# Transposing normalized activations by DMA in place of TensorE in a fused local-attention and gated-MLP kernel

## The chip, the core and the metric

The kernel runs on one core of a Trainium2 chip. A core has a matrix engine (TensorE, PE in the profile, with its weight loads as PEld), a vector engine (VectorE, DVE), an activation engine (ScalarE, ACT), GpSimd (POOL) and SyncE (SP), which here only issues DMAs. Each engine takes its own instructions strictly in order; semaphores order the engines against one another. The metric is the time of one execution on the device in microseconds, the median of several runs.

## What is computed

Input x has 2048 rows of 1024 values (bf16). Each row is normalized (xn), and xn goes through two branches: an attention with 32 heads of 32 values, in which each position looks at 8 earlier positions at distances 0, 2, ..., 14, and a gated MLP of width 3584. The result is x + s * silu(MLP).

```python
def reference(A_x, A_wqkv, A_wo, B_x, B_w1, B_w3, B_w2):
    ...
        qkv = (lambda x, *d: x.transpose(*d))((x @ wqkv).reshape(B, S, 3, H, Dh), 2, 0, 3, 1, 4)
    ...
        logits = jnp.einsum("bhsd,bhswd->bhsw", q, kg) * scale
        logits = jnp.where(mask[None, None, :, :], logits, -1e9)
        attn = _softmax(logits, axis=-1)
        o = jnp.einsum("bhsw,bhswd->bhsd", attn, vg)
    ...
        h = _silu(gate) * up
        out = jnp.einsum("bsf,fd->bsd", h, w2)
    ...
    x = A_x
    xn = _layernorm(x, axis=-1)
    s = _A_ref(xn, A_wqkv, A_wo)
    g = _silu(_B_ref(xn, B_w1, B_w3, B_w2))
    return x + s * g
```

## The kernel before

The 2048 rows are worked on in four chunks of 512 rows (c = 0 to 3), each of four tiles of 128 rows. TensorE contracts over the partition axis, so xn is needed transposed: the tile xnT holds, for each of the 8 blocks of 128 model columns, 128 partitions (columns) by 512 rows. There are two xnT buffers.

For each chunk the program text has these steps, in this order:

- `qkv` (line 143): 24 blocks of queries, keys and values, 8 matmuls each (line 159), with weights wt streamed from a permuted copy wperm in device memory; in chunk 0 they come from tiles pm that were permuted on the chip. ScalarE copies the results to qT, kT and vT (line 170).
- `attention` (line 172): VectorE multiplies qT with shifted kT, once per distance, and adds up (lines 177 to 180); GpSimd's DMAs regroup the sums (line 184); a softmax follows (lines 188 to 201); its result goes back by DMA (line 204); VectorE multiplies it with shifted vT and adds up to oT (lines 211 to 226).
- `wo_proj` (line 229): 64 matmuls of oT with the output weights wa and wb (line 241), copied to s_sb by ScalarE.
- `mlp_up` (line 250): 14 blocks fb of 256 columns. Each loads w1t and w3t (lines 255 and 257) and makes four PSUM tiles of 8 matmuls each (line 264, named gu_fb_k); ScalarE applies Silu to the gate (sg, line 271) and VectorE multiplies it with the other half (ht, line 273). That product frees the PSUM tiles; the pool psum_mm has six.
- `ln_transpose` (line 112) for the next chunk, c + 1: SyncE loads four tiles x_t (line 122, four buffers), VectorE makes the statistics (lines 125 and 126), ScalarE a square root (line 129), VectorE the reciprocal (line 130) and then xn, tile by tile (line 133, two buffers). TensorE transposes each xn tile in eight blocks of 128 columns into a PSUM tile tp (line 139; tp shares a pool of two buffers with wo_proj), and ScalarE copies tp to xnT (line 140).
- `mlp_down_epilogue` (line 294): for each half of the output columns, 112 matmuls into four accumulators (line 324), with w2t streamed through three buffers (line 320), and then the final Silu, product and sum (lines 289 to 292). The last half of chunk 3 has its own order (line 311).

Chunk 0 differs in that its `ln_transpose` runs first of all, tile by tile, and that its first four MLP blocks are made before the loop (lines 332 to 338).

The program text does not fix the order on the engines. A scheduler places each engine's instructions at build time: of those that it takes to be ready, it picks the one that stands earliest in the text (or is marked high priority), and it lets later work move far ahead when its inputs and a buffer are there. That order is then fixed, and an instruction whose input is late on the chip holds all that stand behind it on its engine. All weight and x_t loads are issued by SyncE, in one queue; GpSimd issues the attention's DMAs, x_e and the output.

Of the kernel before, what the change touches and what calls it, by code (L numbers as in the profile page):

```python
# [15 lines left out]
def kernel(  # L16
# [11 lines left out]
    nc = tc.nc  # L28
    P = 128
# [40 lines left out]
    for _ in range(NWARM):  # L70
# [4 lines left out]
        out=ident[:], in_=ident[:], compare_op=ALU.not_equal, fill=1.0,  # L75
# [5 lines left out]
        out=maskb[0:32], in_=maskb[0:32], compare_op=ALU.is_ge, fill=-1.0e9,  # L81
# [30 lines left out]
    def ln_transpose(c, group=NST):  # L112
        xnT = xnT_pool.tile([P, KT, CH], BF16, tag="xnT")
        mv = small.tile([P, NST, nc.vector.BN_AGGR_DIM], FP32, tag="mv")
        rstd = small.tile([P, NST], FP32, tag="rstd")
        for st0 in range(0, NST, group):
            sts = range(st0, st0 + group)
            x_ts = {}
            for st in sts:
                g = c * NST + st  # L120
                x_t = ln.tile([P, D], BF16, tag="x_t", bufs=NST)
                nc.sync.dma_start(out=x_t[:], in_=x_flat[g * P:(g + 1) * P, :])
                stats = small.tile([P, 2, nc.vector.BN_STATS_DIM], FP32, tag="stats")
                for i in range(2):
                    nc.vector.bn_stats(out=stats[:, i, :], in_=x_t[:, i * 512:(i + 1) * 512])  # L125
                nc.vector.bn_aggr(out=mv[:, st, :], in_=stats[:])
                x_ts[st] = x_t
            sl = slice(st0, st0 + group)
            nc.scalar.activation(out=rstd[:, sl], in_=mv[:, sl, 1], func=ACTF.Sqrt, bias=eps_t[:], scale=1.0)
            nc.vector.reciprocal(out=rstd[:, sl], in_=rstd[:, sl])  # L130
            for st in sts:
                xn = ln.tile([P, D], BF16, tag="xn")
                nc.vector.tensor_scalar(
                    out=xn[:], in0=x_ts[st][:], scalar1=mv[:, st, 0:1], scalar2=rstd[:, st:st + 1],
                    op0=ALU.subtract, op1=ALU.mult,
                )
                tp = psum_aux.tile([P, KT, P], BF16, tag="aux")
                for kt in range(KT):
                    nc.tensor.transpose(tp[:, kt, :], xn[:, kt * P:(kt + 1) * P], ident[:])  # L139
                nc.scalar.copy(out=xnT[:, :, st * P:(st + 1) * P], in_=tp[:])  # L140
        return xnT
# [188 lines left out]

    pools = {}
    xnT_cur = ln_transpose(0, group=1)
    hts0 = []
    with tc.tile_pool(name="stage", bufs=1) as stage:
# [4 lines left out]
        for t in range(3):  # L339
            nc.sync.dma_start(  # L340
                out=wperm[:, :, t * NJ:(t + 1) * NJ, :].rearrange("kt kp j p -> kp kt (j p)"),
                in_=pms[t][:].rearrange("kp kt j p -> kp kt (j p)"),
# [9 lines left out]
    for c in range(NCH):  # L352
        if c > 0:
            qkv(c, xnT_cur)
        oT = attention(c)
        s_sb = wo_proj(c, oT)
        if c == 0:
            hts = hts0 + mlp_up(c, xnT_cur, M1B, FT // 2)
        else:
            hts = mlp_up(c, xnT_cur, 0, FT // 2)  # L360
        xnT_next = ln_transpose(c + 1) if c + 1 < NCH else None
        mlp_down_epilogue(c, hts, s_sb)
        xnT_cur = xnT_next
# [30 lines left out]
```

## Time and profile before

| | us |
|---|---|
| median of 3 runs | 841.57 |
| lowest and highest run | 841.38 and 841.77 |
| span of the profiled execution | 841.2 |
| chunk 0 up to the end of its qkv | 0 to 62.6 |
| rest of chunk 0, up to the first line 159 of chunk 1 | 62.6 to 223.7 (161.1) |
| chunk 1 | 223.7 to 427.0 (203.3) |
| chunk 2 | 427.0 to 630.2 (203.2) |
| chunk 3 | 630.2 to 841.2 (211.0) |

The parts overlap on the other engines; they are cut where TensorE begins the projections of the next chunk. The profile is of one execution. In lines of the timeline the columns are start and duration in microseconds, engine, line of the kernel, operation, output<-input, tile shapes and a count; in brackets is the time that the engine stood idle before, and what ended it. "SPq" and "POOLq" are the queues in which these engines issue DMAs; a duration there is the time that the issue holds the queue, and the transfer goes on behind it ("landing" counts from the issue to the last byte).

### The profile page before, as it was taken

How to read it: one execution, taken by the hardware profiler on the slowest of the kernel's cores; microseconds unless marked ns; L12 is line 12 of the kernel's file. 1: busy time of each engine (PE TensorE's matmuls, PEld its weight loads, DVE VectorE, ACT ScalarE, POOL GpSimd, SP SyncE). 2: the span in 40 equal slices, each digit the busy share in tenths (PEclk: the TensorE clock that was granted, in tenths of full speed). 3: DMA queues.
4: the chain of work that ended last, by engine and by line, in shares of the span. 5: the costliest groups of instructions: out<-in, count | busy, mean ns of one | idle time of the engine just before them, and what ended most of it. 6: DMA issues, size and time to landing. Idle time of an engine off the chain costs nothing.

```text
span 841.2 us, 9707 instructions
## 1 busy us (share of the span) xinstructions
PE 819.3 (97%) x3884; PEld 377.0 (45%) x3884; DVE 477.1 (57%) x488; ACT 213.9 (25%) x325; POOL 123.7 (15%) x210
## 2 busy tenths in 40 slices
PE   7999889999999999999999999999999999999995
PEld 5444334444444444444444444444444444444442
DVE  7429946595239835494143955379302693629811
ACT  6742113103343113102233212210403311310120
POOL 1002133003100224002120040401102004120011
PEclk8999999999999999999999999999999999999998
DMA  9999397746595596754675577855476559593320
GB/s 302 314 358 230 102 226 173 190 150 176 130 289 149 153 201 183 177 164 119 193 239 150 148 170 185 202 154 167 114 213 200 151 150 200 159 205 112 109 81 25
DMA packets 208525, 149.54 MB, mean 178 GB/s; under 512 B 7776, under 2 KB 196192, under 8 KB 208480
## 3 DMA queue, kind: packets, MB, share of 16 engines
q1 hardware_dynamic: 201296, 132.14, 57.2%
q0 software_dynamic: 7184, 16.79, 8.0%
q8 instruction: 30, 0.49, 0.3%
q14 instruction: 15, 0.12, 0.1%
HBM read 130.02 MB, written 10.49 MB: 167 GB/s over the span
## 4 chain that ended last, share of the span: by engine, by line
PE 80%; DVE 15%; issue 3%; DMA 1%; ACT 0%; POOL 0%; POOLq 0%; DVEq 0%
PE ps L159 20%; PE ps L241 7%; DVE oT L226 2%; DVE B L225 2%; DVE C L211 2%; DVE B L211 2%; DVE ht L273 1%; DVE prod L177 1%; DMA x_t<-in_A_x_dram 1%; PE tp L139 1%; DVE oT L219 1%; PE acc_1_3_1668 L324 1%; PE acc_1_2_6323 L311 1%; PE acc_1_0_4763 L324 1%; PE acc_0_2_1505 L324 1%
## 5 line engine op out<-in xcount | busy, mean ns | idle before, releaser
L264 PEld LDWEIGHTS <-w3t 128*128 128x128 bf16 x912 | 89.8, 98 | 111.4 <-issue 7.8
L264 PEld LDWEIGHTS <-w1t 128*128 128x128 bf16 x912 | 89.6, 98 | 104.6 <-issue 0.2
L159 PE MATMUL ps<-xnT,wt 128*128 128x512 bf16 x576 | 124.8, 379 | 0.0
L324 PEld LDWEIGHTS <-ht 128*128 128x128 bf16 x784 | 76.4, 98 | 90.0 <-issue 0.2
L177 DVE TENSOR_TENSOR prod<-qT,kT 128x4096 bf16<-128x4096 bf16 x32 | 72.6, 2286 | 41.8 <-ACT kT L170 40.9
L159 PEld LDWEIGHTS <-wt 128*128 128x128 bf16 x576 | 56.3, 98 | 68.0
L290 DVE TENSOR_TENSOR gt<-gt,s_sb 128x512 f32<-128x512 f32 (+1 forms) x33 | 21.6, 673 | 77.0 <-ACT gt L289 64.3
L125 DVE BATCH_NORM_STATS2 stats<-x_t 128x6 f32<-128x512 bf16 x32 | 20.5, 671 | 58.4 <-DMA x_t<-in_A_x_dram 58.4
L204 POOL DMA_DIRECT2D E_persist<-pb x64 | 36.9, 584 | 100.1 <-DVE pb L201 93.3
L292 POOL DMA_DIRECT2D out_dram<-o_t x33 | 18.2, 551 | 205.9 <-DVE o_t L291 204.4
L159 PE MATMUL ps<-xnT,pm 128*128 128x512 bf16 x192 | 41.6, 379 | 0.0
L241 PEld LDWEIGHTS <-oT 128*128 128x128 bf16 x256 | 24.8, 98 | 32.9 <-DVE oT L226 3.4
L178 DVE TENSOR_TENSOR prod<-prod 128x2048 bf16<-128x2048 bf16 x32 | 38.4, 1219 | 0.0
L211 DVE TENSOR_TENSOR B<-E_persist,vT 128x4096 bf16<-128x4096 bf16 x16 | 36.5, 2284 | 0.0
L241 PE MATMUL ps<-wa,oT 128*128 128x512 bf16 x128 | 32.9, 379 | 1.9 <-DVE oT L226 1.9
L241 PE MATMUL ps<-wb,oT 128*128 128x512 bf16 x128 | 32.8, 379 | 0.0
L247 ACT CAST s_sb<-ps 128x512 bf16<-128x512 f32 x32 | 18.8, 586 | 48.5 <-PE ps L241 48.5
L159 PEld LDWEIGHTS <-pm 128*128 128x128 bf16 x192 | 18.8, 98 | 22.4
L291 DVE TENSOR_TENSOR o_t<-gt,x_e 128x512 bf16<-128x512 f32 (+1 forms) x33 | 21.6, 672 | 12.1 <-DMA x_e<-in_A_x_dram 11.8
L170 ACT CAST kT<-ps 128x512 bf16<-128x512 f32 x32 | 18.8, 586 | 36.5 <-PE ps L159 36.5
L226 DVE TENSOR_TENSOR oT<-oT,B 128x4096 bf16<-128x4096 bf16 x12 | 27.5, 2292 | 0.4
L170 ACT CAST vT<-ps 128x512 bf16<-128x512 f32 x32 | 18.7, 586 | 35.4 <-PE ps L159 35.4
(579 smaller groups left out, 1276.3 us busy)
## 6 DMA issues: line engine op xcount, KB each, us to landing
w1t<-in_B_w_dram SPq DMA_DIRECT2D x56, 512.0 KB, 4.3
w3t<-in_B_w_dram SPq DMA_DIRECT2D x56, 512.0 KB, 5.1
w2t<-in_B_w_dram SPq DMA_DIRECT2D x49, 512.0 KB, 3.5
wt<-wperm SPq DMA_DIRECT2D x36, 512.0 KB, 4.3
raw<-in_A_wqkv_dram SPq DMA_DIRECT2D x6, 1024.0 KB, 7.4
wperm<-pm SPq DMA_DIRECT2D x3, 2048.0 KB, 14.8
x_t<-in_A_x_dram SPq DMA_DIRECT2D x16, 256.0 KB, 5.6
wa<-in_A_wo_dram SPq DMA_DIRECT2D x32, 128.0 KB, 4.1
```

The lines of the kernel that those rows point to most:

```text
L159: nc.tensor.matmul(ps[:], lhsT=lhsT, rhs=xnT[:, kt, :], start=(kt == 0), stop=(kt == KT - 1),)
L170: nc.scalar.copy(out=dst, in_=ps[:])
L177: nc.vector.tensor_mul(prod[:], qT[:], kT[:, :, o:o + CH])
L178: nc.vector.tensor_add(prod[:, 0:4, :], prod[:, 0:4, :], prod[:, 4:8, :])
L204: nc.gpsimd.dma_start(out=E[r * 32:(r + 1) * 32, :, sq * P:(sq + 1) * P], in_=pb[sq * 32:(sq + 1) * 32, :, :],)
L211: nc.vector.tensor_mul(dst, E[:, w, :].unsqueeze(1).to_broadcast([P, NJ, CH]), vT[:, :, o:o + CH])
L226: nc.vector.tensor_add(A, A, B[:])
L241: nc.tensor.matmul(ps[:], lhsT=oT[:, j, st * P:(st + 1) * P], rhs=(wa if j < 4 else wb)[:, j % 4, :], start=(j == 0), stop=(j == NJ - 1),)
L264: nc.tensor.matmul(pss[k][:, cs], lhsT=wt[:, kt, i * P:(i + 1) * P], rhs=xnT[:, kt, cs], start=(kt == 0), stop=(kt == KT - 1),)
L290: nc.vector.tensor_mul(gt[:, lc], gt[:, lc], s_sb[:, st, gc])
L291: nc.vector.tensor_add(o_t[:, lc], gt[:, lc], x_e[:, lc])
L324: nc.tensor.matmul(accs[st][:], lhsT=hts[f][:, st * P:(st + 1) * P], rhs=w2t[:, i, :], start=(f == 0), stop=(f == FT - 1),)
```

## The change

For chunks 1 to 3, `ln_transpose` no longer uses TensorE and ScalarE. As soon as a tile of xn is written, SyncE issues one DMA that transposes it on the way from SBUF to SBUF, straight into its 128 columns of xnT. The tile is 128 rows by 1024 columns (256 KB); the destination is 128 partitions by 8 blocks by 128 rows. Chunk 0 keeps its path. Buffers and all else stay.

```diff
@@ -134,6 +134,9 @@
                     out=xn[:], in0=x_ts[st][:], scalar1=mv[:, st, 0:1], scalar2=rstd[:, st:st + 1],
                     op0=ALU.subtract, op1=ALU.mult,
                 )
+                if c > 0:
+                    nc.sync.dma_start_transpose(out=xnT[:, :, st * P:(st + 1) * P], in_=xn[:])
+                    continue
                 tp = psum_aux.tile([P, KT, P], BF16, tag="aux")
                 for kt in range(KT):
                     nc.tensor.transpose(tp[:, kt, :], xn[:, kt * P:(kt + 1) * P], ident[:])
```

## The prediction

> **What bounds the kernel now.** I read the page first, then the chain of waits, then the timeline of TensorE around the transposes, and last what the SyncE queue and VectorE do where chunk 1 is normalized.
>
> ```profile
> span 841.2 us, 9707 instructions
> ...
> PE 819.3 (97%) x3884; PEld 377.0 (45%) x3884; DVE 477.1 (57%) x488; ACT 213.9 (25%) x325; POOL 123.7 (15%) x210
> ...
> PE 80%; DVE 15%; issue 3%; DMA 1%; ACT 0%; POOL 0%; POOLq 0%; DVEq 0%
> ```
>
> TensorE is busy for 819.3 of 841.2 us and carries 80% of the chain that ends last. So a TensorE instruction that is taken out shortens the kernel by its place in the queue, if nothing else becomes late. The span lies 0.37 us below the median of the runs (841.57); I make the sums against the span and add them to the median.
>
> **What the change removes.** The timeline of TensorE shows the four transposed tiles of chunk 1 between the output projection and the rest of the down projection:
>
> ```profile
> 207.85 1.03 PE L241 MATMUL ps<-wb,oT 128*128 128x512 bf16 x4
> 208.71 0.61 PE L139 MATMUL tp<-ident,xn 128*128 128x128 bf16 x8
> 209.16 0.38 PE L324 MATMUL acc_1_0_1665<-w2t,ht 128*128 128x512 bf16 x1
> 209.55 0.61 PE L139 MATMUL tp<-ident,xn 128*128 128x128 bf16 x8
> 209.99 0.38 PE L324 MATMUL acc_1_1_1666<-w2t,ht 128*128 128x512 bf16 x1
> ...
> 223.48 0.38 PE L324 MATMUL acc_1_3_1668<-w2t,ht 128*128 128x512 bf16 x1
> 223.69 1.03 PE L159 MATMUL ps<-xnT,wt 128*128 128x512 bf16 x4
> ```
>
> The second column is a duration with its pipeline tail; what an instruction costs the queue is the distance to the next start. Eight transposes take 209.16 - 208.71 = 0.45 us, some 55 ns each. From 208.71 to 223.69 are 14.98 us, with 60 matmuls of the down projection in them. These follow one another every 0.2157 us (four in 0.863 us), so they need 12.94 us, and the transposes with the small waits around them cost 2.04 us. The same sum gives 26.75 us less 114 x 0.2157 for chunk 2 (400.21 to 426.96) and for chunk 3 (603.47 to 630.22): 2.16 us each. Removed in all: **6.4 us** of TensorE's queue. No idle time of TensorE is there to swallow it: from 223.7 to 630.2 us it is busy for 405.2 of 406.5 us. VectorE's order is paced by TensorE's results in these chunks (it waits for each gate-and-up pair), so it moves along.
>
> The Trainium skill would make this larger: "TensorE: Matmul & The Clock Gate", Part 4, measures about 275 ns for a transpose in a kernel. 96 of them at that price would be an estimated 26 us; the pitch in this trace is 55 ns, and the measurement decides.
>
> The 12 ScalarE copies (line 140, 1.04 us each) go too. I cost them at nothing: ScalarE is busy 25%, and nobody but the transposes waited for these copies (1.1 us in all, in chunk 0, which keeps them).
>
> **What it adds.** Twelve DMAs of 256 KB, SBUF to SBUF, issued on SyncE's queue, where all weights are issued too. No row shows a transposing DMA; bounds come from these rows of the answers for x_t, w2t and pm:
>
> ```profile
> L122 SPq DMA_DIRECT2D x_t<-in_A_x_dram x16: 340/428/6183, 0.7 to 419.7; - x16
> ...
> DMA to landing us min/median/max: 2.6/5.6/15.3
> ...
> L340 SPq DMA_DIRECT2D wperm<-pm x3: 1736/1911/3211, 34.0 to 37.9; - x3
> ```
>
> Hold of the queue: 0.43 us (x_t, the same 256 KB) to 1.91 us (wperm<-pm, which reads SBUF, 2 MB). I take the middle, 1.2 us. Landing: 2.6 to 15.3 us, and I take x_t's median of 5.6. Moved bytes are no issue: 3.1 MB beside 149.5 MB.
>
> The skill disagrees with itself here. "VectorE: DVE Perf Modes", The three transpose paths, gives 1309 ns for 128x128 by DMA and advises TensorE; eight in a row are an estimated 10.5 us for each of our tiles. "Advanced Engine Details and Errata", X-Bar Transpose (TRN2), says that a transposing DMA is as fast as a plain one, by which the x_t row would hold unchanged. With 10.5 us the slower case below gains weight; nothing in the trace of before shows which holds.
>
> For their results there is much time: chunk 1's projection starts at 223.7 us and two of its tiles are normalized at 102 us. So the landing itself is not on the path. What counts is order: SyncE and VectorE each run their queue in order, and the added wait (the transpose waits for xn) stands in SyncE's queue ahead of weights. The xn tile has two buffers, so tiles 2 and 3 wait on VectorE for a landing instead of for TensorE. In chunk 0 this already hurts:
>
> ```profile
> 101.86 1.00 DVE L133 TENSOR_SCALAR xn<-x_t,mv,rstd 128x1024 bf16<-128x1024 bf16 x2
> 102.78 0.68 DVE L273 TENSOR_TENSOR ht<-sg,gu_5_1_999 128x512 bf16<-128x512 bf16 x1
> 105.78 1.28 DVE L125 BATCH_NORM_STATS2 stats<-x_t 128x6 f32<-128x512 bf16 x2 [2.32 <-DMA x_t<-in_A_x_dram]
> 109.46 0.69 DVE L125 BATCH_NORM_STATS2 stats<-x_t 128x6 f32<-128x512 bf16 x1 [2.40 <-DMA x_t<-in_A_x_dram]
> 110.74 0.67 DVE L273 TENSOR_TENSOR ht<-sg,gu_5_3_1001 128x512 bf16<-128x512 bf16 x1
> ```
>
> ```profile
> 102.44 1.66 SPq L122 DMA_DIRECT2D x_t<-in_A_x_dram  x2
> 104.22 0.38 SPq L255 DMA_DIRECT2D w1t<-in_B_w_dram  x1
> ```
>
> ```profile
> 106.81 1.89 PE L264 MATMUL gu_7_0_1094<-xnT,w1t 128*128 128x512 bf16 x8
> 111.46 3.27 PE L264 MATMUL gu_7_1_1095<-xnT,w3t 128*128 128x512 bf16 x8 [2.76 <-DVE ht L273]
> ```
>
> SyncE waits for xn until 102.44 us before it loads the next x_t; VectorE stands at the statistics of that x_t; the product ht behind them is late; TensorE has no free PSUM tile and stands for 2.76 us, and its next eight matmuls take 3.27 us in place of 1.73 (the granted clock from 90 to 115 us is 0.93). One such event costs 2.76 + 1.54 = 4.3 us.
>
> In the changed kernel the two transposes of tiles 0 and 1 go out between xn and these x_t loads: 2 x 1.2 = 2.4 us (bounds 0.9 and 3.8) by which this event grows. The weights behind them, at 104.2 us, then land near 111.7 us by the 5.1 us of a w3t load, and are used at 118.2 us. In the down projection a w2t tile comes free every 16 x 0.2157 = 3.45 us, and with three buffers there are 6.9 - 3.5 = 3.4 us to spare. Two transposes there fit; four in a row (4.8 us) would cost 1.4 us in a chunk. The last w2t tile is thus the next to be late.
>
> Sum: 841.57 - 6.4 + 2.4 = **837.6 us**.
>
> **The rivals.**
>
> *More events in chunk 0 (slower).* Now that xn is freed by a DMA and no longer by TensorE at 209 us, the rest of chunk 1's normalization and part of chunk 2's can run between 103 and 160 us, in VectorE's queue between the ht products. Each landing that VectorE meets in order (tiles 2 and 3 of xn, the x_t loads after them, xn of chunk 2) can be an event of 4.3 us. For it: the row above, the late 11.8 us that SyncE waited for xn, and the square root on ScalarE, which moves in among the Silu's. Against it: from 115 us on, VectorE waits 2.77 us in every 3.45 us. It decides from 1.5 events on (6.4 / 4.3). Three events in place of the one lengthening: 841.57 - 6.4 + 12.9 = 848.1 us; four, 852.4.
>
> *The gain is given back (no change).* One and a half events, or one and four transposes amid the w2t loads of both chunks (4.3 + 2.8 = 7.1): 841.6 to 842.3 us. What can be told from no change for this kernel is about 0.2%, 1.7 us.
>
> *The stall is resolved (much faster).* A new order of the queues may load x_t away from the ht products. Then 6.4 + 4.3 go: 830.9 us. For it: all four x_t buffers come free long before they are needed. Against: VectorE is just as late with chunk 0's attention there.
>
> *The transposes stay on TensorE's path in another form:* the next chunk's projection waiting for a landing. Against it are the 120 us between xn and its use; it would need a tile of xn that is normalized after 218 us.
>
> **How the numbers follow.** Forecast 0.42, much faster 0.08, no change 0.12, slower 0.38. Faster than 839.9 us: 0.50; within: 0.12; slower than 843.3 us: 0.38. The forecast's own range goes from 835.2 (the transposes cost nothing) to 839.9 us. The whole range is 831 (the stall resolved) to 852 us (four events); I leave 0.03 below and 0.12 above it, for landings near the 15.3 us of the slowest x_t.
>
> **What would show it.** Right: TensorE's 64-matmul projection followed directly by line 324, each chunk from 223.7 us on some 2.1 us shorter than now (203.3 and 203.2 us between the starts of line 159), the transposes' hold on SyncE between 0.4 and 1.9 us, no wait of line 159 for xnT, and the chunk-0 part (62.6 to 223.7 us, 161.1 us) at about 161.1 - 2.0 + 2.4 us. Wrong: that part over 165 us, with TensorE waiting for ht of VectorE, which in turn waits for xn or x_t; or waits of line 324 for w2t. A landing of many microseconds, with weight loads behind it, would make the bounds themselves wrong.

## The result, and the profile after

The changed kernel takes **855.08 us** (median of 4 runs, 854.13 to 856.27) against 841.48 us for the kernel before beside it: ratio 1.0165, 95% interval 1.0148 to 1.0182. It is slower. The forecast of 837.6 us and its whole range are missed. Single runs of some kernels below were far slower than the rest (991 to 4965 us); the times given leave them out.

The lines of the page after that answer to those shown of before (in the changed kernel every line behind 136 stands 3 lower in the text, so L264 is now L267 and L324 is L327):

```profile
span 852.9 us, 9448 instructions
...
PE 816.3 (96%) x3714; PEld 372.9 (44%) x3788; DVE 475.4 (56%) x488; ACT 202.8 (24%) x313; POOL 123.4 (14%) x210
...
PE 72%; DVE 19%; issue 3%; DMA 3%; SPq 1%; another core or an unknown queue 1%; ACT 1%; POOL 0%; POOLq 0%; DVEq 0%
...
L267 PE MATMUL gu<-xnT,w3t 128*128 128x512 bf16 (+1 forms) x894 | 215.2, 382 | 10.5 <-DVE ht L276 9.5
```

TensorE has less to do (816.3 us against 819.3) and the span is longer all the same: it stands for 9.5 us waiting for the product ht. DMA has 3% of the chain that ends last, against 1% before, and SyncE's queue appears in it. The starts of the projection (L162) tell which stretch lost:

| stretch | before | after | forecast |
|---|---|---|---|
| up to the end of chunk 0's projection | 62.6 | 63.2 | 62.6 |
| rest of chunk 0 | 161.1 | 172.4 | 161.5 |
| chunk 1 | 203.3 | 205.3 | 201.1 |
| chunk 2 | 203.2 | 201.1 | 201.1 |
| chunk 3 | 211.0 | 210.9 | 211.0 |

Against the forecast 10.9 us are lost in chunk 0 and 4.2 us in chunk 1; chunk 2 is as foretold. Now the queues between 100 and 130 us, in the timeline after. First SyncE's queue, where the second column is the time for which an issue holds the queue (in a row of several, from the start of the first to the end of the last; a wait for an input stands ahead of a row):

```profile
103.00 3.43 SPq L138 DMA_TRANSPOSE xnT<-xn  x2
106.50 2.51 SPq L122 DMA_DIRECT2D x_t<-in_A_x_dram  x2
109.12 1.03 SPq L258 DMA_DIRECT2D w1t<-in_B_w_dram  x1
110.66 4.30 SPq L138 DMA_TRANSPOSE xnT<-xn  x1
115.08 0.50 SPq L260 DMA_DIRECT2D w3t<-in_B_w_dram  x1
115.69 4.13 SPq L138 DMA_TRANSPOSE xnT<-xn  x1
119.87 1.04 SPq L122 DMA_DIRECT2D x_t<-in_A_x_dram  x2
```

Before, the first two x_t loads went out at 102.44 us and w1t at 104.22. Now they leave at 106.50 and 109.12, and the last two x_t loads stand behind two further transposes, which hold the queue for 4.30 and 4.13 us each, until 119.87. VectorE meets all this in order, and so does ScalarE, whose square root of chunk 2 was put between two Silus (one line of each view):

```profile
108.66 0.55 DVE L133 TENSOR_SCALAR xn<-x_t,mv,rstd 128x1024 bf16<-128x1024 bf16 x1 [4.62 <-DMA xnT<-xn]
...
123.62 1.88 DVE L125 BATCH_NORM_STATS2 stats<-x_t 128x6 f32<-128x512 bf16 x3 [6.57 <-DMA x_t<-in_A_x_dram]
...
173.59 0.55 DVE L133 TENSOR_SCALAR xn<-x_t,mv,rstd 128x1024 bf16<-128x1024 bf16 x1 [5.41 <-DMA xnT<-xn]
```

```profile
127.04 0.30 ACT L129 ACTIVATE rstd<-mv,eps_t 128x4 f32<-128x4 f32 x1 [10.42 <-DVE mv L126]
```

The figure in brackets is the time for which the engine stood before the instruction. VectorE stands for a landing of a transpose (4.62), for x_t (6.57), and ScalarE for the statistics (10.42); the products ht behind them are late, and TensorE has no free PSUM tile:

```profile
98.75 3.08 PE L267 MATMUL gu<-xnT,w3t 128*128 128x512 bf16 x7 [2.80 <-DVE ht L276]
...
114.68 3.00 PE L267 MATMUL gu<-xnT,w3t 128*128 128x512 bf16 x8 [4.00 <-DVE ht L276]
...
126.14 3.26 PE L267 MATMUL gu<-xnT,w3t 128*128 128x512 bf16 x8 [2.71 <-DVE ht L276]
...
189.03 18.76 PE L327 MATMUL acc<-w2t,ht 128*128 128x512 bf16 x85 [0.93 <-DMA w2t<-in_B_w_dram]
...
210.74 1.78 PE L244 MATMUL ps<-wa,oT 128*128 128x512 bf16 x4 [2.94 <-DVE oT L229]
```

```profile
401.41 1.34 PE L244 MATMUL ps<-wa,oT 128*128 128x512 bf16 x3 [3.17 <-DVE oT L229]
```

After each of the first three stalls a row of seven or eight matmuls takes 3.00 to 3.26 us in place of 1.89. The first of these stalls was there before as well, with no slow matmuls behind it:

```profile
98.18 1.89 PE L264 MATMUL gu_5_3_1001<-xnT,w3t 128*128 128x512 bf16 x8 [2.80 <-DVE ht L273]
```

The third wait of VectorE (173.59 us, an xn of chunk 2) stands ahead of the product of the softmax with vT, which starts at 174.32 us in place of 160.34 (7.8 us of this because the products ht ahead of it are late already, 6.2 us by the wait); so oT is late, and the output projection waits for 2.94 us at 210.74, and for 3.17 us in chunk 1. VectorE's wait is not made by the hold of a transpose alone: the transposes of chunk 2 leave late themselves:

```profile
167.82 4.60 SPq L138 DMA_TRANSPOSE xnT<-xn  x2
```

Their xn were written from 127.69 us on. But six loads of wt stand ahead of them in SyncE's queue, and these wait for 18.1 us in all for the gate-and-up matmuls to free their buffers, until chunk 0's last block is done; the xnT buffer that the transposes fill is in use as long. So VectorE comes to the third xn while the first two are still on their way. The stretch from 100 to 130 us in numbers, before and after (columns: length; TensorE's busy time and its instructions; granted clock; busy share of the DMA engines; GB/s):

```profile
100.00:130.00 30.00, 27.24 (x121) 0.94 0.92 193
```

```profile
100.00:130.00 30.00, 23.02 (x88) 0.86 0.91 179
```

By the records there are 33 matmuls fewer in 30 us, which at 0.2157 us each are 7.1 us. The starts of the groups of eight agree: from the first stall to 131 us the lag behind the kernel before grows by 7.2 us. The slow matmuls behind the first stall are 1.4 us of it, the second event is 1.5 us dearer than the one that was there before, and the third, with 4.2 us, is new. Measured against before, with the transposes' 2.0 us counted as saved, chunk 0 lost 13.3 us; the other 6.1 us are the wait for w2t (1.1 us) and that for oT with the slow matmuls behind it (5.0 us).

### The profile page after: what moved, and what is told of

Its sections match the earlier page's. It is cut to its first block, busy times and chain, and to the rows that moved or that the text cites. A ratio compares the mean times of both kernels' runs of the same rounds, so it can differ in the third digit from the quotient of the medians.

```text
span 852.9 us, 9448 instructions
## 1 busy us (share of the span) xinstructions
PE 816.3 (96%) x3714; PEld 372.9 (44%) x3788; DVE 475.4 (56%) x488; ACT 202.8 (24%) x313; POOL 123.4 (14%) x210
## 3 DMA queue, kind: packets, MB, share of 16 engines
q1 hardware_dynamic: 213968, 135.29, 58.2%
## 4 chain that ended last, share of the span: by engine, by line
PE 72%; DVE 19%; issue 3%; DMA 3%; SPq 1%; another core or an unknown queue 1%; ACT 1%; POOL 0%; POOLq 0%; DVEq 0%
PE gu L267 37%; PE ps L162 19%; PE acc L327 7%; PE ps L244 7%; DVE oT L229 3%; DVE B L228 3%; DVE B L214 3%; DVE C L214 3%; DMA x_t<-in_A_x_dram 2%; DVE ht L276 1%; PE acc L314 1%; DMA xnT<-xn 1%; DVE prod L180 1%; DVE stats L125 1%; DVE oT L222 1%
## 5 line engine op out<-in xcount | busy, mean ns | idle before, releaser
L267 PE MATMUL gu<-xnT,w3t 128*128 128x512 bf16 (+1 forms) x894 | 215.2, 382 | 10.5 <-DVE ht L276 9.5
L267 PE MATMUL gu<-xnT,w1t 128*128 128x512 bf16 (+1 forms) x894 | 211.6, 377 | 1.1 <-issue 0.2
L327 PE MATMUL acc<-w2t,ht 128*128 128x512 bf16 x769 | 169.6, 379 | 1.6 <-DMA w2t<-in_B_w_dram 0.9
L276 DVE TENSOR_TENSOR ht<-sg,gu 128x512 bf16<-128x512 bf16 x112 | 76.6, 685 | 125.0 <-PE gu L267 116.6
L267 PEld LDWEIGHTS <-w3t 128*128 128x128 bf16 x912 | 90.5, 99 | 117.0 <-issue 14.5
L267 PEld LDWEIGHTS <-w1t 128*128 128x128 bf16 x912 | 89.9, 99 | 105.6 <-issue 1.8
L274 ACT ACTIVATE sg<-gu 128x512 bf16<-128x512 f32 x112 | 66.5, 597 | 285.4 <-PE gu L267 248.8
L162 PE MATMUL ps<-xnT,wt 128*128 128x512 bf16 x565 | 124.2, 379 | 0.6
L327 PEld LDWEIGHTS <-ht 128*128 128x128 bf16 x784 | 76.7, 98 | 93.6 <-issue 1.4
L162 PEld LDWEIGHTS <-wt 128*128 128x128 bf16 x576 | 56.3, 98 | 68.0
L292 ACT ACTIVATE gt<-acc 128x512 f32<-128x512 f32 (+1 forms) x33 | 18.2, 586 | 178.5 <-PE acc L327 152.7
L187 POOL DMA_DIRECT2D L<-E_persist x64 | 37.2, 588 | 76.5 <-DVE E_persist L183 64.7
L295 POOL DMA_DIRECT2D out_dram<-o_t x33 | 18.1, 549 | 198.7 <-DVE o_t L294 198.7
L162 PE MATMUL ps<-xnT,pm 128*128 128x512 bf16 x188 | 41.2, 379 | 0.2
```

The costliest lines, as they stand in the source:

```text
L162: nc.tensor.matmul(ps[:], lhsT=lhsT, rhs=xnT[:, kt, :], start=(kt == 0), stop=(kt == KT - 1),)
L187: nc.gpsimd.dma_start(out=L4[sq * 32:(sq + 1) * 32, r, :, :], in_=E[r * 32:(r + 1) * 32, :, sq * P:(sq + 1) * P],)
L267: nc.tensor.matmul(pss[k][:, cs], lhsT=wt[:, kt, i * P:(i + 1) * P], rhs=xnT[:, kt, cs], start=(kt == 0), stop=(kt == KT - 1),)
L274: nc.scalar.activation(out=sg[:], in_=pss[2 * i][:], func=ACTF.Silu)
L276: nc.vector.tensor_mul(ht[:], sg[:], pss[2 * i + 1][:])
L327: nc.tensor.matmul(accs[st][:], lhsT=hts[f][:, st * P:(st + 1) * P], rhs=w2t[:, i, :], start=(f == 0), stop=(f == FT - 1),)
```

## The experiments

Two theories stood at the start. **ORDER**: with xn freed early, normalization runs ahead into chunk 0's products, and the waits on VectorE and ScalarE that this puts into their order cost, whoever transposes. **DMA**: the transposing DMAs themselves cost, by their hold of SyncE's queue and their landing. The kernel before took 840.6 to 840.8 us beside these runs. All kernels lie some 1.8 us above their span; the profiled execution of before (a span of 841.2 us) was one of its longer ones, the spans of its later runs were mostly near 839.

**The DMAs added to the kernel before.** TensorE's path stays and the DMAs write the same result beside it.

```
+                if c > 0:
+                    nc.sync.dma_start_transpose(out=xnT[:, :, st * P:(st + 1) * P], in_=xn[:])
                 tp = psum_aux.tile([P, KT, P], BF16, tag="aux")
```

> The kernel before, with the 12 transposing DMAs added beside the TensorE transposes and ScalarE copies (both write the same values into xnT). xn tiles are still held until TensorE has read them, so later chunks' normalization does not run ahead. Theory ORDER (the loss comes from normalization work of later chunks that runs ahead into chunks 0 and 1 and stands in VectorE's and ScalarE's queues): the added DMAs cost only their hold of SyncE's queue ahead of the x_t loads in chunk 0, so 841.5 to 846 us. Theory DMA (the transposing DMA itself is dear, by its hold, its landing or by blocking weights): most of the 13.6 us appear, 850 us or more.

Measured: 850.17 us, ratio 1.0106 (1.0089 to 1.0123). That is what DMA gave. Its trace comes from a second run, further below.

**A plain copy in place of the transpose**, the same bytes from xn to xnT.

```
-nc.sync.dma_start_transpose(out=xnT[:, :, st * P:(st + 1) * P], in_=xn[:])
+nc.sync.dma_start(out=xnT[:, :, st * P:(st + 1) * P], in_=xn[:].rearrange("p (k r) -> p k r", k=KT))
```

> The changed kernel with a plain SBUF-to-SBUF copy of the same 256 KB in place of each transposing DMA, so xnT of chunks 1 to 3 is left untransposed. Theory ORDER: the run-ahead stays, so the time stays near the changed kernel, 850 to 858 us. Theory DMA: the plain copy's shorter hold takes most of the loss away, 836 to 845 us.

Measured: 842.06 us, ratio 1.0017 (1.0008 to 1.0027); such a copy holds the queue for 0.78 us in the median. The copies are not free: TensorE waits for ht for 11.1 us in all and is busy for 23.73 us from 100 to 130 us, so that all of the 6.4 us saved is lost again. That speaks for DMA, but weakly: the scheduler also placed the square root one Silu later and a product ht ahead of the statistics, so more than the kind of DMA differs.

**The run-ahead alone**, TensorE's transposes with four xn buffers, so that nothing has to wait for TensorE to free one (space for them from the warm-up tile and a softmax tile that share buffers).

```
-                xn = ln.tile([P, D], BF16, tag="xn")
+                xn = ln.tile([P, D], BF16, tag="xn", bufs=NST)
```

> The kernel before with four xn buffers in place of two (room for them is made by two small tiles that share memory), TensorE transposes kept, no transposing DMA. x_t tiles come free at 102 us, so that the loads and statistics of chunk 2 run ahead into chunk 0. Theory ORDER: slower than before without any transposing DMA, 844 to 852 us. Theory DMA: as before, 840 to 843 us.

Measured: 841.83 us, ratio 1.0011 (1.0002 to 1.0021). Run-ahead without the DMAs costs about 1 us. ORDER alone falls.

**The DMAs for chunk 3 alone** (`if c == 3`).

> The transposing DMA for chunk 3 alone; chunks 1 and 2 keep TensorE. Its four transposes then fall behind TensorE's last transposes of chunk 2, at 400 us and later, where VectorE has little to do. If a transposing DMA costs nothing where no urgent work stands behind it, one chunk's 2.2 us are gained: 838 to 839.5 us. If it costs as such, no gain: 840.5 us or more.

Measured: 838.76 us, ratio 0.9978 (0.9969 to 0.9988), with chunk 2, which carries them, at 201.1 us. Four transposes there bring their 2.1 us and harm nothing.

**The changed kernel, held back.** The x_t loads of chunk 1 may not be issued before the w3t load of the 13th block of chunk 0, those of chunks 2 and 3 not before the 7th wt load of the chunk before. The transposes follow their x_t, so they are held back too.

```
+                with tc.issue_after(marks[c]) if c in marks else nullcontext():
+                    nc.sync.dma_start(out=x_t[:], in_=x_flat[g * P:(g + 1) * P, :])
...
+                if b == 6:
+                    marks[c + 1] = ld.ins
...
+            if c == 0 and fb == 12:
+                marks[1] = ld.ins
```

> The changed kernel with its normalization paced: SyncE issues the x_t loads of chunk 1 only behind the w3t load of block 12 of chunk 0, and those of chunk 2 and 3 only behind the seventh wt load of the chunk before. All 12 transposing DMAs stay. Theory ORDER: the waits in chunk 0 vanish, together with the second one of the kernel before (4.3 us), and the 6.4 us of TensorE's transposes are gained: 831 to 836 us. Theory DMA: the 12 transposes still cost what they cost, 845 us or more.

Measured: **833.19 us**, ratio 0.9907 (0.9890 to 0.9924), faster than both kernels. The same twelve DMAs are no harm here, so DMA in its plain form falls as well. In the trace, the line of the transposes and its waits (here L141):

```profile
L141 SPq DMA_TRANSPOSE xnT<-xn x12: 1231/1268/4571, 140.4 to 440.3; - x12
...
  DVE xn L136: 20.1, 6
...
DMA to landing us min/median/max: 3.1/3.8/7.5
```

```profile
148.02 0.55 DVE L136 TENSOR_SCALAR xn<-x_t,mv,rstd 128x1024 bf16<-128x1024 bf16 x1 [5.78 <-DMA xnT<-xn]
```

VectorE waits longer for landings than in the changed kernel (20.1 us against 14.5), one of them for 5.78 us amid the last products, and TensorE has no wait of 0.85 us or more behind 100 us. What a wait costs is set by what stands behind it. From 100 to 130 us TensorE is now busy throughout:

```profile
100.00:130.00 30.00, 29.89 (x138) 1.00 0.79 186
130.00:170.00 40.00, 39.79 (x183) 1.00 0.98 232
```

**The same holding back with TensorE's transposes.**

> The kernel before (TensorE transposes, ScalarE copies) with the same pacing of x_t loads as the paced version, no transposing DMA. It parts the 7.6 us that the paced version gained. If TensorE's freed queue is worth 6.4 us as the prediction had it, this lies 6 us over the paced version, at 837 to 840 us. If the pacing alone made the gain, it lies at 832 to 834 us.

Measured: 839.62 us, ratio 0.9985 (0.9974 to 0.9996). The pair gives the worth of the change by itself: 839.62 - 833.19 = 6.4 us, the 6.4 of the prediction. The runs of either kernel spread over some 3 us, but the lowest of the two differ by 6.4 us and the highest by 6.3.

**Is it the wait for landings?** The changed kernel with the four xn buffers: no tile waits for the landing of another of its chunk, and VectorE's waits for landings fall from 14.5 to 6.0 us.

> The changed kernel with four xn buffers in place of two (room by the same two small tiles sharing memory), so that no tile of a chunk waits on VectorE for the landing of another tile of its chunk. Theory LANDING (the loss is VectorE waiting in its queue for a transposing DMA to land): 838 to 846 us. Theory RUN-AHEAD (the loss is the loads, statistics and square root of chunks 2 and 3 standing in the queues of chunks 0 and 1 at all): 850 us or more, since more of them run ahead.

Measured: 852.80 us, ratio 1.0143 (1.0127 to 1.0159). LANDING falls as the main cause. With the run on four buffers without DMAs this makes a pair: 841.8 with TensorE, 852.8 with the DMAs, though they save 6.4 us. The trace shows the loss moved to the weights: all four transposes leave in a row, ahead of w1t, and TensorE stands for the weights themselves.

```profile
102.30 9.71 SPq L138 DMA_TRANSPOSE xnT<-xn  x4
112.52 0.97 SPq L258 DMA_DIRECT2D w1t<-in_B_w_dram  x1
```

```profile
120.59 3.60 PE L267 MATMUL gu<-xnT,w1t 128*128 128x512 bf16 x8 [6.85 <-DMA w1t<-in_B_w_dram]
```

**Holding back a part.** Chunks 2 and 3 alone:

> The paced version with chunk 1 left as in the changed kernel: only the x_t loads of chunks 2 and 3 are held back. VectorE's order in chunk 0 is that of the changed kernel up to the last xn of chunk 1, and nothing of chunks 2 and 3 stands behind it. LANDING: the two waits for chunk 1's own transposes stay and stop TensorE once (4.0 us and 2.3 us of slower matmuls in the changed kernel), so 838 to 842 us. RUN-AHEAD: with chunks 2 and 3 gone from the queue nearly all is gained, 831 to 836 us.

Measured: 838.70 us, ratio 0.9980 (0.9967 to 0.9994). And chunk 1 alone:

> The changed kernel with the loads of x_t held back for chunk 1 alone, behind the load of w3t of the 13th block of chunk 0; chunks 2 and 3 run ahead as they like. Holding back chunks 2 and 3 alone gave 838.7 us, all three 833.2 us. If the two savings add (16.4 and 5.5 us), this gives 849 to 850 us. If it is the meeting of chunk 1's transposes with chunk 2's loads in the middle of chunk 0's products that costs, either pacing takes most of the cost away: 834 to 841 us.

Measured: 846.48 us, ratio 1.0062 (1.0045 to 1.0079), 8.6 us less than the changed kernel. The two savings (16.4 and 8.6) add to 3.1 us more than that of both (21.9), so no single meeting of the two chunks makes most of the loss. With chunk 1 late, chunk 2's transposes stand among the w2t loads, where they wait for an xn behind chunk 0's attention:

```profile
177.21 1.24 SPq L141 DMA_TRANSPOSE xnT<-xn  x1
178.50 0.57 SPq L125 DMA_DIRECT2D x_t<-in_A_x_dram  x1
179.87 1.24 SPq L141 DMA_TRANSPOSE xnT<-xn  x1
181.21 0.64 SPq L328 DMA_DIRECT2D w2t<-in_B_w_dram  x1
```

```profile
185.32 6.86 PE L332 MATMUL acc<-w2t,ht 128*128 128x512 bf16 x31 [2.10 <-DMA w2t<-in_B_w_dram]
```

**Another queue.** The transposes issued by ScalarE, so that SyncE has loads alone:

```
-                    nc.sync.dma_start_transpose(out=xnT[:, :, st * P:(st + 1) * P], in_=xn[:])
+                    nc.scalar.dma_start_transpose(out=xnT[:, :, st * P:(st + 1) * P], in_=xn[:])
```

> The changed kernel with its twelve transposing DMAs issued by ScalarE's queue; SyncE's queue then holds loads alone, as before the change. HOLD theory (the cost comes from the transposes standing in SyncE's queue ahead of the loads of x_t and the weights): x_t and the weights of chunk 0's gate-and-up land as early as before, TensorE's waits for ht in chunk 0 shrink from 9.5 us to under 5, and the time is 836 to 845 us; what is left is ScalarE's own hold between Silus. VECTOR theory (the cost comes from VectorE's and ScalarE's own order, statistics and square root run ahead among the products ht, whatever queue issues the transposes): 850 us or more.

Measured: 858.11 us, ratio 1.0189 (1.0161 to 1.0217). HOLD as I had put it, SyncE's queue and no other, falls; the trace shows why VECTOR does not follow from it. In the timelines of ScalarE's queue, of VectorE and of TensorE:

```profile
108.91 11.95 ACTq L138 DMA_TRANSPOSE xnT<-xn  x2
120.97 1.08 ACT L274 ACTIVATE sg<-gu 128x512 bf16<-128x512 f32 x2 [14.40 <-DVE ht L276]
```

```profile
118.73 0.55 DVE L133 TENSOR_SCALAR xn<-x_t,mv,rstd 128x1024 bf16<-128x1024 bf16 x1 [9.25 <-DMA xnT<-xn]
```

```profile
120.59 3.36 PE L267 MATMUL gu<-xnT,w3t 128*128 128x512 bf16 x8 [12.09 <-DVE ht L276]
```

From 108.91 to 120.86 us ScalarE is taken up by two transposes, with the Silus behind them, and TensorE stands for 12.09 us. The two issues themselves are 2.64 and 1.55 us of this. In between ScalarE stands for the fourth xn, and VectorE writes that late because it waits 9.25 us for the landing of an earlier transpose (landings reach 15.6 us here). So what has moved with the transposes is less their hold than the wait in front of them.

The loads of x_t of chunks 1 to 3 issued by GpSimd instead (`nc.gpsimd.dma_start` for `c > 0`):

> The changed kernel with the loads of x_t for chunks 1 to 3 issued by GpSimd's queue; the transposes stay on SyncE's, ahead of the weights. HOLD theory in its narrow form (the late x_t behind the transposes is what makes the statistics and the products ht late): x_t lands without the transposes ahead of it, VectorE no longer waits for x_t near 112 and 123 us, 836 to 845 us. If the weights behind the transposes are what counts, TensorE waits for w1t or w3t and the time stays at 848 us or more. VECTOR theory: 850 us or more.

Measured: 843.94 us, ratio 1.0044 (1.0027 to 1.0062), within what HOLD gave. But chunk 1's transposes now stand at 49 to 67 us, and the whole order with them, so this run tells less than it seems to; TensorE's longest wait for ht is 6.9 us at 109 us.

**The DMAs moved, the run-ahead kept.** Four xn buffers, and only chunk 1's transposes, not its x_t loads, held back behind the 13th block:

```
+                    with tc.issue_after(marks[c]) if c in marks else nullcontext():
+                        nc.sync.dma_start_transpose(out=xnT[:, :, st * P:(st + 1) * P], in_=xn[:])
```

> The changed kernel with four xn buffers, and with the transposing DMAs of chunk 1 (only these, not the loads of x_t) held back behind the load of w3t of the 13th block of chunk 0. The loads of x_t and the statistics and square roots of chunks 1 and 2 still run ahead in the middle of chunk 0's products, as in the run with four xn buffers alone, which took 852.8 us. PLACE theory (what costs is that the transposing DMAs are issued and carried between 100 and 130 us, where the DMA engines are at over 90% and loads that are due stand behind them): TensorE's busy time from 100 to 130 us returns to 27 us or more, and the time is 832 to 841 us. RUN-AHEAD theory (what costs is VectorE's and ScalarE's early work on chunk 2): 848 us or more.

Measured: 843.73 us, ratio 1.0038 (1.0025 to 1.0051). RUN-AHEAD falls: statistics and square root of chunk 2 stand amid the products as before (ScalarE waits 8.62 us for them), and the time is 9.1 us less than with the transposes in the early place. PLACE has its first half, 27 us or more of TensorE's work from 100 to 130 us, and misses the time by 2.7 us. The windows and SyncE's queue show where that went:

```profile
100.00:130.00 30.00, 28.36 (x126) 0.97 0.99 210
130.00:170.00 40.00, 34.62 (x150) 0.96 1.02 212
```

```profile
131.74 8.13 SPq L141 DMA_TRANSPOSE xnT<-xn  x4
139.97 1.95 SPq L261 DMA_DIRECT2D w1t<-in_B_w_dram  x1
142.02 1.42 SPq L124 DMA_DIRECT2D x_t<-in_A_x_dram  x1
```

The same event happens again where the transposes now are: four hold the queue for 8.13 us, chunk 3's x_t loads stand behind them, and TensorE waits three times, 5.3 us in all (0.81, 1.15, 3.32).

**The first experiment again, for its trace.**

> The kernel before the change with the twelve transposing DMAs added beside TensorE's transposes, again (850.3 us the first time), for its trace. PLACE theory: in this kernel too the transposes stand in SyncE's queue from 102 us ahead of loads of x_t and weights, TensorE's busy time from 100 to 130 us falls from 27.2 us to under 25, and its waits there are over 5 us in all. If the 9.5 us over the kernel before are lost elsewhere (in the down projection, waiting for w2t behind transposes), TensorE is busy for 27 us there and waits after 160 us: over 5 us in all.

Measured: 850.17 us, ratio 1.0117 (1.0094 to 1.0141). This is the event in its simplest form, one alone. SyncE, VectorE, TensorE in the timeline, and the window:

```profile
102.65 3.90 SPq L138 DMA_TRANSPOSE xnT<-xn  x2
106.61 2.04 SPq L122 DMA_DIRECT2D x_t<-in_A_x_dram  x2
```

```profile
113.51 1.29 DVE L125 BATCH_NORM_STATS2 stats<-x_t 128x6 f32<-128x512 bf16 x2 [9.83 <-DMA x_t<-in_A_x_dram]
114.71 0.67 DVE L275 TENSOR_TENSOR ht<-sg,gu 128x512 bf16<-128x512 bf16 x1
```

```profile
115.44 3.57 PE L266 MATMUL gu<-xnT,w3t 128*128 128x512 bf16 x8 [6.52 <-DVE ht L275]
```

```profile
100.00:130.00 30.00, 23.21 (x94) 0.83 0.90 176
```

Two transposes delay the x_t loads from 102.44 to 106.61 us (4.17 us), the product ht behind the statistics from 110.74 to 114.71 (3.97), and TensorE's wait grows from 2.76 to 6.52 us (3.76). One delay runs through SyncE, VectorE and TensorE almost undiminished. PLACE is met on all its numbers; no long wait follows in the down projection (0.59 us for w2t at most).

## Why the prediction was wrong

**The saving was right.** TensorE's 6.4 us are there: 6.4 in the pair held back (to the tenth by luck, as the runs spread), and 2.1 us in chunk 2 of the changed kernel itself. ScalarE's copies were worth nothing, as said.

**The price of one hold was right, but for a quiet queue.** I took 1.2 us, with bounds of 0.43 and 1.91. Alone a transpose holds the queue for 1.24 us; in the changed kernel the row has a minimum of 1.237, a median of 1.748 and a maximum of 4.302 us, well above the bound, and the first two at 103 us take 3.43 together, 3.90 in the kernel of the last run. The event was to grow by 2.4 us with 3.8 as the upper bound. In the kernel of the last run it grew by about 4. In the changed kernel the x_t loads are as late (102.44 to 106.50 us), but TensorE's wait grew by 1.24 us alone (2.76 to 4.00), as TensorE was itself 2.0 us later by then.

**The failed step is the term "+ 2.4 us" as the whole price.** It counted one event that grows, left the new ones to the rival, and had no term for a late oT. The reason against the rival was that from 115 us on VectorE waits 2.77 us in every 3.45 us. That slack comes in gaps of 2.77 us: a wait of 6.6 or 5.4 us in one piece is more than one such gap, and each of these (as the wait of 4.6 us ahead of 115 us) held products, or the softmax's product, that TensorE was due to need. The runs show +17.5 us against the forecast, and about 22 us that holding back recovers. In the changed kernel's stretches the 17.5 us were 10.9 us in chunk 0 (13.3 less the 2.4 that the forecast had) and 4.2 us in chunk 1; the rest is 0.6 us of the start and the long profiled execution of before.

**The rival named the mechanism and its price.** Events of 4.3 us, three for 848.1 and four for 852.4 us. Of the events of the trace the new one cost 2.71 + 1.5 us (the wait and the eight slow matmuls), the price; the one that grew has 4.00 + 1.3 us. It also named the square root among the Silus, and xn of chunk 2. What it lacked is the second leg: VectorE's late start on oT, and with it the waits of 2.94 and 3.17 us in the output projection, which with the slow matmuls behind them are 5.0 us in chunk 0 and 4.2 us in chunk 1. The prediction had put nothing there: it let VectorE's order move along with TensorE's. So that four events at 4.3 us (852.4 us) come near the result is in part luck. I gave it 0.38 against 0.42, and left 0.12 above 852 us; the result is there.

**The smaller steps.** That the weights from 104 us on would be in time was right for the changed kernel, with w1t gone out at 109.1, and wrong as soon as four transposes went in a row (6.85 us of wait for w1t). That w2t is the next to be late was right: 0.93 us here, 2.10 and 1.60 us with chunk 1 alone held back. That moved bytes are no issue was not tested: the DMA engines are busy 0.91 of the time in that stretch, 0.92 before, but landings reach 10.0 us, against 7.5 at most in the kernel held back.

**What stays open.** How much of the loss is the hold of a queue and how much the crowded DMA engines was not separated. In the single event above the hold accounts for all of the delay, but it is 3.90 us for two transposes, where two alone take 2.5; why a hold grows to this, or to 4.30 us, no run shows. Which part the lower clock has, apart from the stalls that precede it, was not tried.

## What to carry to other kernels

A DMA that waits for a computed tile is a blocking instruction of the queue it stands in: before moving work from an engine to such a DMA, list what stands ahead of it and behind it on that queue in the busiest stretch, and follow each late item to the engine that needs it. Moving it to ScalarE's queue moved the blocking to the Silus; what helped was to hold the whole chain back (load, statistics, transpose) to a stretch where nobody behind it is due, which turned 855 into 833 us. And slack of so much in every so much is no cover for one long wait.

## What the runs showed of the hardware

A transposing DMA of 256 KB holds the issuing queue for 1.24 us when nothing else delays it, three times the 0.43 us of a plain load of the same size. Its landing takes a median of 3.8 us in the kernel held back (x_t: 5.1 us there). The Trainium skill, "VectorE: DVE Perf Modes", The three transpose paths, has 1309 ns for one 128x128 by DMA; eight of them would be an estimated 10.5 us, which these landings do not bear out, and no run here has a single one. The same skill's "Advanced Engine Details and Errata", X-Bar Transpose (TRN2), has a transposing DMA as fast as a plain one, which agrees with the landing and not with the hold.

A transpose takes more of the DMA engines than a load of as many bytes. With a queue of their own on ScalarE (q10; q1 has all of SyncE's loads; columns: packets, MB, share of the 16 engines' span), the page has:

```profile
q1 hardware_dynamic: 201296, 132.14, 56.6%
...
q10 hardware_dynamic: 12672, 3.15, 2.5%
```

That is 0.43% for a MB of loads and 0.79% for a MB of transposes, 1.85 times as much. That it is the transposing is not shown: on SyncE's queue the plain copies from xn to xnT come out no cheaper (q1 has 59.2% of 842.2 us with them, 58.2% of 852.9 us with the transposes, 57.2% of 841.2 us with neither).

The same stall of 2.8 us near 98 us, which nearly every kernel here has, was followed by seven or eight matmuls in 1.67 to 1.89 us in eight profiled executions and in 3.08 to 3.44 us in five. From 97 to 103 us the granted clock is 1.00 in the eight and 0.72 in the five. The eight are all those that resumed at 98.40 us or before, the five all those that resumed at 98.71 us or later: in these thirteen, whether a stall of the same length lowers the clock goes with when it falls, and some 1.4 us hang on it. Why was not tried.
